# First quarter loads and splits of a seven-product mixing stage issued under the end of the stage before it

## The chip, the cores and the metric

The kernel runs on one NeuronCore of a Trainium2 chip. The metric is the device time of one execution in microseconds (us). Engines are named as in the profile: PE (TensorE matmul), PEld (its weight loads), DVE (VectorE), ACT (ScalarE), POOL (GpSimd) and SP (SyncE, which here only issues transfers).

## The reference

Three blocks follow each other, all in float32 (cut to what matters):

```python
Y = soft_threshold(rfft(x, axis=1) @ W + b)            # complex W, lam = 0.01
x = irfft(Y, n=3072, axis=1)                           # (4, 3072, 256)
h = relu(x @ w_in); u, v = h[..., :512], h[..., 512:]
v_n = (v - mean(v)) / sqrt(var(v) + 1e-6)
v_s = einsum('ts,bsd->btd', w_spatial, v_n) + b_spatial[None, :, None]
x = ((u * v_s) @ w_out).reshape(4 * 3072, 256)
out = (s * relu(x @ w2_in) ** 2 + b) @ w2_out          # 2048 hidden columns
```

## The kernel before

Every float32 operand of a product is split into a high and a low half (`_hl` tiles), and a product is three passes: high by high, high by low, low by high. ACT casts the high half, DVE subtracts to get the low half.

The program has three stages, written one after the other; each engine gets its instructions in the order of the Python code, and nothing reorders them.

`attention` is the filter: a 3072-point transform in steps (`s1`, `g_stage`), the channel product (`mix`), and two inverse steps (`g2_stage`, `s3`). Beside the last inverse step `s3` runs `v_product`, which makes the 96 row blocks of `v` (tile `vr`; the product's PSUM tile is `ps_vp`), normalises them three at a time (`bn`, `rs`, L583 to L601) and stores them to DRAM as `vn`. When the main loop is over, 40 of the 128 `s3` steps are left; the loop at L678 to L685 does them with the remaining `v_product`s. I call it the **tail**. In it SP issues the loads `v_f` (L276) and the stores `yd` (L465), POOL the stores `vn`.

`mixing` multiplies the 3072x3072 matrix with `vn` by a seven-product scheme on 2x2 blocks, nested twice: 7 outer times 7 inner products of 6 steps, 294 steps `n` of 24 matmuls (L834) each. Operands are kept as quarters, SBUF tiles `a11` to `b22`, six pieces each (`a` pieces 384 KB, `b` pieces 256 KB). Lines L858 and L859 issue the first 48 piece loads. A step's operands are split two steps ahead (`high`, `low`), three splits are held (`bufs=3`), and sums of quarters (`sums`) are made three steps ahead. The accumulators `acc` take all eight PSUM banks: `acc` 0 stands where `ps_g` was, 1 where `pm` was, 2 on `pa`, 3 on `py`; `v_product` of the tail uses `pm` and `pa`. Between steps one of 40 weight pieces is converted from float64 (`convert_half`, tiles `c_w`: a load on SP, nine DVE operations L143 to L158, one ACT copy L155, a store `cd`); every third step may start one, and it is worked off two steps later (L887 to L891).

`output` forms 16 blocks: it sums the outer products read back from DRAM (`combine`, tiles `m`), multiplies by `u` (`u_product`, L983 and L986), and runs the two layers (L1020, L1041). Its 20 weight tiles `w` come from `cd`; before, POOL issues all of them at L917, behind its stores of `md`.

Of the kernel before, what the change touches and what calls it, by code (L numbers as in the profile page):

```python
# [19 lines left out]
NB = 4  # L20
# [204 lines left out]
    return float(np.array([bits], np.uint32).view(np.float32)[0])  # L225


def attention(tc, nc, x, w_r, w_i, b_r, b_i, c_f, c_b, c_g, c_v, c_s, zd, vd, yd, vn, chunks, cd, nb=NB):


    left, right = Pools(tc, "left"), Pools(tc, "right")
# [6 lines left out]
    pg = left("a_pg", 1, space=PSUM)  # L238
    pm = left("a_pm", 2, space=PSUM)
    pa = left("a_pa", 2, space=PSUM)  # L240
    py = left("a_py", 2, space=PSUM)
    ch = Chains()

    cf = const.tile([N1, 2 * N1], F32R, name="cf")
# [237 lines left out]
    y_hl = {}  # L482
    chunks_ready = [0]

    root = const.tile([128, 1], F32, name="root")
    nc.vector.memset(root, 1.0)
    nc.scalar.sqrt(root, root)
    nc.gpsimd.dma_start(out=cf, in_=c_f)
# [181 lines left out]
    def s3_more():  # L670
        nonlocal s3_done
        if s3_done < 32 * nb:
# [14 lines left out]
    right.close()  # L687
    left.close()

# [16 lines left out]
FIRST_USE = {"a12": 0, "b21": 0, "a21": 1, "a22": 1, "b12": 1, "b11": 1, "a11": 2, "b22": 2}  # L706


def mixing(tc, nc, ws, vn, md, sd, convert_half):


# [1 line left out]

    left, right = Pools(tc, "left"), Pools(tc, "right")
    ring = left("m_ring", 3)
    stage = left("m_stage", 2)
    quarters = left("m_quarters", 1)
    keep = right("m_keep", 1)
    accs = left("m_acc", 1, space=PSUM)
    q = {}  # L720
    QUARTERS = ("a11", "a12", "a21", "a22", "b11", "b12", "b21", "b22")
    for name in ("a12", "b21", "a21", "a22", "b12", "b11", "b22", "a11"):
        n = TQ if name[0] == "a" else 512
        for i in range(NS):
            q[name, i] = quarters.tile([128, n], F32, tag=f"{name}{i}", name=name)
    PASSES = ((0, 0), (0, 1), (1, 0))
    outer = list(OUTER)

# [12 lines left out]
    def load(g, name, i):  # L741
        first, then = OUTER[outer[g]][0 if name[0] == "a" else 2:][:2]
        t = q[name, i]
        nc.sync.dma_start(out=t, in_=source(first, name, i))
        if then is None:
            return
        op, second, kept = then
        n = t.shape[1]
        s = stage.tile([128, n], F32, tag="st_" + name[0], name="st_" + name[0], bufs=3)
# [31 lines left out]
    def sums(n):  # L781

        p, i = INNER[n // NS % 7], n % NS
        a11, a12, a21, a22, b11, b12, b21, b22 = (q[x, i] for x in QUARTERS)
        if p == 2:
            a, b = a12, b21
        elif p == 5:
            add(a21, a21, a22)
            sub(b12, b12, b11)
            a, b = a21, b12  # L790
        elif p == 3:
            sub(a21, a21, a11)
            a, b = ring.tile([128, TQ], F32, tag="s4", name="s4", bufs=2), b22
            sub(a, a12, a21)
        elif p == 1:
            a, b = a11, b11
        elif p == 6:
            sub(b12, b22, b12)
            sub(b11, b12, b11)
            sub(b22, b21, b12)  # L800
            a, b = a21, b12
        elif p == 7:
            sub(a21, a22, a21)
            a, b = a21, b11
        else:
            a, b = a22, b22
        term["a", n], term["b", n] = a, b
# [13 lines left out]
            todo.extend((g + 1, FIRST_USE[x], n % NS, x) for x, last in LAST.items() if last == at)  # L821

    acc = {}

    def multiply(n):
        p, i = INNER[n // NS % 7], n % NS
        a, b = hl.pop(("a", n)), hl.pop(("b", n))
        fresh = p in (2, 5, 1, 4)
        for d in range(4):
            if i == 0 and fresh:  # L830
                acc[d] = accs.tile([128, 2, 512], F32, tag=f"acc{d}", name="acc")
# [6 lines left out]
    kept = {}  # L838

    def keep_tile(k, d):  # L840
        return keep.tile([128, 2, TH], F32, tag=f"k{k}{d}", name="kept")

    def evacuate(n, d):
        g, at = divmod(n // NS, 7)
# [10 lines left out]
            nc.scalar.copy(t, ps)  # L855

    total = len(outer) * 7 * NS
    for n in sorted(((u, i, x) for x, u in FIRST_USE.items() for i in range(NS))):  # L858
        load(0, n[2], n[1])  # L859
    for n in range(2):  # L860
        sums(n)
        for kind in "ab":
            high(kind, n)
            low(kind, n)
    sums(2)
    conversion = []
    for n in range(total):
        now[0] = n
        multiply(n)
        ends = n % NS == NS - 1  # L870
        if n + 2 < total:
            high("a", n + 2)
            high("b", n + 2)
        if n + 3 < total:
            sums(n + 3)
        if ends:
            evacuate(n, 0)
            evacuate(n, 1)
        if n + 2 < total:
            low("a", n + 2)  # L880
            low("b", n + 2)
            freed(n + 2)
        if ends:
            evacuate(n, 2)
            evacuate(n, 3)
        outer_sums(3)
        if conversion and (todo or n % 3 == 2):  # L887
            conversion.pop()()
        loads()
        if not conversion and not added and not todo and n % 3 == 0:  # L890
            conversion = [x for x in [convert_half(stage)] if x]  # L891
    while True:
        for x in conversion:
            x()
        conversion = [x for x in [convert_half(stage)] if x]
        if not conversion:
            break
    left.close()
    right.close()


def output(tc, nc, yd, md, chunks, cd, bs, s_in, b_in, out):


    left, right = Pools(tc, "left"), Pools(tc, "right")
    late = left("o_late", 2)
    mpool = left("o_m", 9)
    work = left("o_work", 2)
    wts_late = right("o_wl", 1)
# [120 lines left out]
    def layer2(n, k):  # L1030
        s = sq_t.pop((n, k))
        if k == 0:
            oacc[n] = accs.tile([128, 2, 512], F32, tag="oacc", name="oacc")
        ps = oacc[n]
        for e in range(2):
            ff = 2 * k + e
            w = w2[8 + ff // 2]
            for h in range(2):
                o = (ff % 2) * 256 + h * 128
                for c, (a, i) in enumerate(PASSES):  # L1040
                    nc.tensor.matmul(ps[:, h, 0:TH], w[:, a, o:o + 128], s[:, i, e, :],  # L1041
                                     start=ff == 0 and c == 0, stop=ff == 2 * NP - 1 and c == 2)
        if k == NP - 1:
            del oacc[n]
            b, o = where(n)
            t = work.tile([128, 2, TH], F32, tag="o_sb", name="o_sb")
# [26 lines left out]
    wo = [weight(4 + k) for k in range(2)]  # L1073
    w2 = [weight(6 + j) for j in range(16)]
# [8 lines left out]
    load_terms(1)  # L1083
    fetch(1)
    out_product(0)
    sums = combine(1)
    steps = [(n, k) for n in range(len(blocks)) for k in range(NP)]
# [35 lines left out]
def network(ctx, tc, ins, out):  # L1123
# [24 lines left out]
        return lambda: [step() for step in convert(nc, c_tile, raw, cd[j][:, :, h * 256:(h + 1) * 256], 256)]  # L1148
    with tc.manual_schedule():
        attention(tc, nc, ins['x'], ins['w_r'], ins['w_i'], ins['b_r'], ins['b_i'],  # L1150
                  ins['c_f'], ins['c_b'], ins['c_g'], ins['c_v'], ins['c_s'], zd, vd, yd, vn, chunks, cd)
        mixing(tc, nc, ins['moe_w_spatial'], vn, md, sd, convert_half)
        output(tc, nc, yd, md, chunks, cd, ins['moe_b_spatial'], ins['moe2_s'], ins['moe2_b'], out)


# [23 lines left out]
```

## Time and profile before

| what | us |
|---|---|
| median of 3 runs | 3241.53 (3240.82 to 3249.85) |
| the profiled execution, its own time | 3237.02 |
| its span, first to last instruction | 3235.2 |
| PE busy | 3090.4 (96%) |
| DVE busy | 2306.8 (71%) |

The span is 1.8 us shorter than the execution's own time, which is 4.5 us under the median. PE is close to full on average; where it is not is read from its timeline. The tail runs from about 475 to 562 us, `mixing` from 569 to 1856 us, `output` from there to the end.

### The profile page before, as it was taken

Reading aid. Unit: us, or ns where it says so; the run is one execution under the profiler, and the core shown is the slowest. Engines: PE = TensorE matmul, PEld = TensorE weight load, DVE = VectorE, ACT = ScalarE, POOL = GpSimd, SP = SyncE. Lnnn points to the kernel's source line nnn. Section 1 sums busy time; section 2 is a strip of 40 time slices with the busy share of each in tenths; the row PEclk is TensorE's granted clock in tenths of the full one; section 3 lists DMA queues with packets and bytes.
Section 4 is the critical chain, followed back from the end, with each engine's and each line's share of the span. In section 5 each row is a group of like instructions: output and inputs, shape, how many; then the busy total and the mean of one; then the engine's idle time right before and its main releaser. Section 6 shows DMA issues by size and latency. Waiting matters only on the chain.

```text
span 3235.2 us, 46499 instructions
## 1 busy us (share of the span) xinstructions
PE 3090.4 (96%) x17960; PEld 3013.2 (93%) x17960; DVE 2306.8 (71%) x3493; ACT 1426.1 (44%) x2241; POOL 396.3 (12%) x508
## 2 busy tenths in 40 slices
PE   7989997798999999999999989999999999999999
PEld 5888985798999999999999979999999999999999
DVE  4877988687878888888878655556666666656564
ACT  4776766333434333443434333444444444444433
POOL 2665534012000210000000100000000000000000
PEclk9999999899999999999999999999999999999999
DMA  7987655689465966467471441111111111110210
GB/s 232 290 266 226 225 178 201 228 289 365 137 208 161 341 248 220 163 198 277 141 250 33 156 140 50 64 54 64 54 64 54 64 54 64 49 65 29 72 44 15
DMA packets 230518, 488.30 MB, mean 151 GB/s; under 512 B 22356, under 2 KB 116376, under 8 KB 230296
## 3 DMA queue, kind: packets, MB, share of 16 engines
q1 hardware_dynamic: 195528, 347.67, 32.4%
q0 software_dynamic: 34768, 137.67, 11.6%
q8 instruction: 140, 2.29, 0.3%
q14 instruction: 82, 0.67, 0.1%
HBM read 322.72 MB, written 162.53 MB: 150 GB/s over the span
## 4 chain that ended last, share of the span: by engine, by line
PE 44%; issue 39%; DVE 8%; POOL 4%; ACT 3%; DMA 1%; POOLq 0%; SPq 0%; ACTq 0%; DVEq 0%
PE oacc L1041 15%; PE ps_h L1020 14%; PE ps_o L1001 4%; PE ps_u L983 4%; PE ps_m L406 3%; PE ps_vp L570 2%; POOL md L852 2%; DVE m L951 1%; DVE r L1025 1%; PE ps_z L332 1%; ACT q_hl L1026 1%; POOL s L755 1%; POOL t L755 1%; PE ps_g L359 1%; PE ps_y L454 1%
## 5 line engine op out<-in xcount | busy, mean ns | idle before, releaser
L834 PE MATMUL acc<-a_hl,b_hl 128*128 128x384 f32 x7056 | 1240.7, 337 | 52.7 <-ACT b_hl L812 25.2
L834 PEld LDWEIGHTS acc<-a_hl,b_hl 128*128 128x128 f32 x7056 | 1234.3, 189 | 59.2 <-ACT b_hl L812 25.9
L1020 PE MATMUL ps_h<-x_hl,w 128*128 128x384 f32 x3072 | 576.7, 337 | 1.6 <-ACT x_hl L1004 0.9
L1041 PE MATMUL oacc<-q_hl,w 128*128 128x384 f32 x3072 | 576.3, 337 | 0.0
L1020 PEld LDWEIGHTS ps_h<-x_hl,w 128*128 128x128 f32 x3072 | 538.2, 188 | 2.5 <-ACT x_hl L1004 1.2
L1041 PEld LDWEIGHTS oacc<-q_hl,w 128*128 128x128 f32 x3072 | 538.5, 188 | 0.2
L812 ACT CAST a_hl<-a 128x768 fp32r<-128x768 f32 x252 | 210.9, 837 | 532.2 <-PE acc L834 450.3
L1027 DVE TENSOR_TENSOR q_hl<-r,q_hl 128x768 fp32r<-128x768 f32 x256 | 245.3, 958 | 230.8 <-ACT q_hl L1026 230.8
L1025 DVE TENSOR_TENSOR r<-r 128x768 f32<-128x768 f32 x256 | 244.7, 956 | 216.0 <-ACT r L1024 216.0
L1026 ACT CAST q_hl<-r 128x768 fp32r<-128x768 f32 x256 | 213.8, 835 | 314.3 <-DVE r L1025 314.3
L1024 ACT ACTIVATE r<-ps_h 128x768 f32<-128x768 f32 x256 | 207.7, 811 | 301.7 <-PE ps_h L1020 300.6
L816 DVE TENSOR_TENSOR a_hl<-a,a_hl 128x768 fp32r<-128x768 f32 x252 | 240.3, 953 | 134.9 <-ACT a_hl L812 133.6
L816 DVE TENSOR_TENSOR b_hl<-b,b_hl 128x512 fp32r<-128x512 f32 x294 | 201.0, 684 | 0.0
L812 ACT CAST b_hl<-b 128x512 fp32r<-128x512 f32 x294 | 181.1, 616 | 0.0
L570 PE MATMUL ps_vp<-win,y_hl 128*128 128x512 f32 x576 | 155.2, 406 | 18.3 <-ACT v_sb L437 15.0
L983 PE MATMUL ps_u<-y_hl,w 128*128 128x384 f32 x768 | 148.7, 344 | 21.6 <-DVE m L986 14.2
L852 POOL DMA_DIRECT2D md<-kept x112 | 60.4, 540 | 827.6 <-DVE kept L851 823.6
L983 PEld LDWEIGHTS ps_u<-y_hl,w 128*128 128x128 f32 x768 | 137.2, 193 | 25.3 <-DVE m L986 16.7
L1001 PE MATMUL ps_o<-g,w 128*128 128x384 f32 x768 | 140.0, 338 | 1.7 <-DVE g L991 1.1
L570 PEld LDWEIGHTS ps_vp<-win,y_hl 128*128 128x128 f32 x576 | 103.1, 192 | 40.5 <-ACT v_sb L437 16.8
L1001 PEld LDWEIGHTS ps_o<-g,w 128*128 128x128 f32 x768 | 134.0, 188 | 2.7 <-DVE g L991 1.6
L990 ACT CAST g<-m 128x768 fp32r<-128x768 f32 x64 | 53.4, 835 | 157.0 <-DVE m L986 134.1
(138 smaller groups left out, 3749.8 us busy)
## 6 DMA issues: line engine op xcount, KB each, us to landing
a<-in_moe_w_spatial_dram SPq DMA_DIRECT2D x144, 384.0 KB, 4.8
b<-vn SPq DMA_DIRECT2D x168, 256.0 KB, 6.1
md<-kept POOLq DMA_DIRECT2D x112, 384.0 KB, 5.5
m<-md SPq DMA_DIRECT2D x56, 768.0 KB, 5.9
st_a<-in_moe_w_spatial_dram SPq DMA_DIRECT2D x72, 384.0 KB, 6.4
vn<-vr POOLq DMA_DIRECT2D x96, 256.0 KB, 3.8
s<-a POOLq DMA_DIRECT2D x48, 384.0 KB, 5.9
x_f<-in_x_dram SPq DMA_DIRECT2D x32, 384.0 KB, 5.8
```

The source lines that it names most:

```text
L570: nc.tensor.matmul(ps, y[:, a, k, o:o + 128], win[k][:, w, :], start=c == 0, stop=c == 5)
L812: nc.scalar.copy(s[:, 0, :], t)
L816: sub(s[:, 1, :], term.pop((kind, n)), f(s)[:, 0, :])
L834: nc.tensor.matmul(acc[d][:, h, 0:TH], b[:, m, d * 128:(d + 1) * 128], a[:, w, h * TH:(h + 1) * TH], start=fresh and i == 0 and c == 0, st ...
L983: nc.tensor.matmul(ps[:, d, 0:TH], win[k][:, a, o:o + 128], y[:, w, k, :], start=c == 0, stop=c == 5)
L1001: nc.tensor.matmul(ps[:, h, 0:TH], wo[k // 2][:, a, o:o + 128], g[:, w, k, :], start=c == 0, stop=c == 11)
L1020: nc.tensor.matmul(ps[:, e, 0:TH], w[:, a, o:o + 128], x[:, i, j, :], start=c == 0, stop=c == 5)
L1024: nc.scalar.activation(r, ps[:, :, 0:TH], AF.Relu)
L1025: nc.vector.tensor_mul(r, r, r)
L1026: nc.scalar.copy(s[:, 0], r)
L1027: nc.vector.tensor_sub(s[:, 1], r, f(s)[:, 0])
L1041: nc.tensor.matmul(ps[:, h, 0:TH], w[:, a, o:o + 128], s[:, i, e, :], start=ff == 0 and c == 0, stop=ff == 2 * NP - 1 and c == 2)
```

## The change

`mixing` is called from inside `attention` and returns an object with three parts. `prefetch` issues one quarter load per turn of the tail loop, 36 of the 48 (all but `a11` and `b22`), into the left side of SBUF, which `attention` closes before its tail. `split_first` sums and splits one step's operands; the tail loop calls it on each turn that ends with 93 or 95 row blocks of `v` started. `run` does the rest. The first conversion is started at step 6 and not at step 0. In `output` the weights `w2` to `w12` move from POOL's queue to SP's, seven of them into space that the quarters of the last product held, and `split(0)` is written ahead of `combine(0)`.

```diff
     tail[0] = True
+    left.close()
+    stage = follow()
     while v_done[0] < NV:
+        stage.prefetch()
         s3_more()
...
+        if v_done[0] in (NV - 3, NV - 1):
+            stage.split_first()
     ch.flush()
     right.close()
-    left.close()
+    banks.close()
+    return stage
...
+    first = sorted((u, i, x) for x, u in FIRST_USE.items() for i in range(NS))
+    begun = [0]
+
+    def prefetch():
+        if first and first[0][2] != "a11":
+            _, i, x = first.pop(0)
+            load(0, x, i)
+
+    def split_first():
+        n = begun[0]
+        begun[0] += 1
         sums(n)
         for kind in "ab":
             high(kind, n)
             low(kind, n)
...
+        while begun[0] < 2:
+            split_first()
+        while first:
+            _, i, x = first.pop(0)
+            load(0, x, i)
+        sums(2)
...
-        if not conversion and not added and not todo and n % 3 == 0:
+            if n >= 6 and not conversion and not added and not todo and n % 3 == 0:
...
     def weight(j):
-        t = (wts_late if j >= 13 else wts).tile([128, 2, 512], F32R, tag=f"w{j}", name=f"w{j}")
-        nc.gpsimd.dma_start(out=t, in_=cd[j])
+        pool = wts_late if j >= 13 else wts_mid if j >= 6 else wts
+        t = pool.tile([128, 2, 512], F32R, tag=f"w{j}", name=f"w{j}")
+        (nc.gpsimd if j >= 13 else nc.sync).dma_start(out=f(t) if j < 13 else t, in_=cd[j])
...
-    load_terms(0)
     fetch(0)
     win = [weight(2 + k) for k in range(2)]
+    load_terms(0)
     wo = [weight(4 + k) for k in range(2)]
...
+    split(0)
     for step in combine(0):
         step()
-    split(0)
```

What SP issues in the tail before, from its middle to the first quarter loads of `mixing`:

```order
L465 DMA yd_68<-y_sb 128x2x384
L276 DMA v_f<-vd_64 96x512 x2
L465 DMA yd_68<-y_sb 128x2x384 x3
L744 DMA a_7447<-in_moe_w_spatial_dram 128x768
L744 DMA b_7453<-vn_69 128x512
```

And in the changed program, one period of the same tail:

```order
L466 DMA yd_68<-y_sb 128x2x384
L758 DMA a_6332<-in_moe_w_spatial_dram 128x768
L758 DMA b_6368<-vn_69 128x512
L277 DMA v_f<-vd_64 96x512
L758 DMA b_6362<-vn_70 128x512
L758 DMA a_6357<-in_moe_w_spatial_dram 128x768
L277 DMA v_f<-vd_64 96x512
L466 DMA yd_68<-y_sb 128x2x384
```

Four quarter loads now stand in each period of two `v_f` loads and one `yd` store. The second place is ACT at the end of the tail, before; the `vr` rows of L608 empty the PSUM tiles of the last `v_product`s:

```order
L608 ACTIVATE vr<-ps_vp 128x512
L611 ACTIVATE rs<-rs 128x3
L608 ACTIVATE vr<-ps_vp 128x512
L599 ACTIVATE vr<-vr,rs 128x512 x2
L608 ACTIVATE vr<-ps_vp 128x512 x2
```

ACT at the same place in the changed program, where the numbers of `a` tell the step:

```order
L609 ACTIVATE vr<-ps_vp 128x512
L826 CAST a_hl<-a_6343 128x768
L826 CAST b_hl<-b_6349 128x512
L612 ACTIVATE rs<-rs 128x3
L826 CAST a_hl<-a_6344 128x768
L826 CAST b_hl<-b_6350 128x512
L609 ACTIVATE vr<-ps_vp 128x512
L600 ACTIVATE vr<-vr,rs 128x512 x2
L609 ACTIVATE vr<-ps_vp 128x512
L826 CAST a_hl<-a_6345 128x768
L826 CAST b_hl<-b_6351 128x512
L609 ACTIVATE vr<-ps_vp 128x512
```

Three pairs of casts have moved ahead of the last three `vr` rows (the loop passes the 93 mark twice and the 95 mark once); the third pair, `a_6345`, is cast again later, since `run` splits step 2 itself. The third place is DVE at the start of `output`, before:

```order
L851 TENSOR_TENSOR kept<-acc,kept 128x768 x4
L1075 MEMSET ones 128x2
L951 TENSOR_TENSOR m<-m 128x768
L953 TENSOR_TENSOR m<-m,bias 128x768
L951 TENSOR_TENSOR m<-m 128x768
L953 TENSOR_TENSOR m<-m,bias 128x768
L969 TENSOR_TENSOR y_hl<-y_f,y_hl 128x768
L986 SCALAR_TENSOR_TENSOR m<-ps_u,m 128x768
```

DVE there in the changed program:

```order
L866 TENSOR_TENSOR kept<-acc,kept 128x768 x4
L1116 MEMSET ones 128x2
L1008 TENSOR_TENSOR y_hl<-y_f,y_hl 128x768
L990 TENSOR_TENSOR m<-m 128x768
L992 TENSOR_TENSOR m<-m,bias 128x768
L990 TENSOR_TENSOR m<-m 128x768
L992 TENSOR_TENSOR m<-m,bias 128x768
L1025 SCALAR_TENSOR_TENSOR m<-ps_u,m 128x768
```

The low half of `y` now comes before the four sums of `m`; the eight rows are otherwise the same.

## Rows read from the trace of the kernel before

**Rows 1.** Timeline of PE, 555 to 650 us: start, length, what [idle before].

```profile
558.24 3.94 PE L570 MATMUL ps_vp<-win,y_hl 128*128 128x512 f32 x16 [0.26 <-DVE y_hl L475]
569.11 22.94 PE L834 MATMUL acc<-a_hl,b_hl 128*128 128x384 f32 x120 [6.94 <-ACT b_hl L812]
...
610.28 1.01 PE L834 MATMUL acc<-a_hl,b_hl 128*128 128x384 f32 x2 [18.23 <-ACT b_hl L812]
612.13 38.12 PE L834 MATMUL acc<-a_hl,b_hl 128*128 128x384 f32 x204 [0.84 <-DVE a_hl L816]
```

**Rows 2.** Timeline of PE, the last stretch of mixing.

```profile
1607.08 248.50 PE L834 MATMUL acc<-a_hl,b_hl 128*128 128x384 f32 x1428 [0.73 <-DVE kept L851]
```

**Rows 3.** Timeline of ACT around the second gap.

```profile
608.57 0.41 ACT L155 CAST c_w<-c_w 128x256 fp32r<-128x256 f32 x1 [27.61 <-DVE c_w L149]
608.88 0.83 ACT L812 CAST a_hl<-a 128x768 fp32r<-128x768 f32 x1
609.62 0.61 ACT L812 CAST b_hl<-b 128x512 fp32r<-128x512 f32 x1
```

**Rows 4.** Timeline of DVE around the second gap.

```profile
607.05 0.29 DVE L143 TENSOR_SCALAR c_w<-c_w 128x256 uint32<-128x256 uint32 x1 [25.02 <-DMA c_w<-in_moe_w_in_dram]
...
609.65 0.95 DVE L788 TENSOR_TENSOR a<-a,a 128x768 f32<-128x768 f32 x1
```

**Rows 5.** Timeline of SP's queue: first quarter load, first conversion load.

```profile
556.76 0.50 SPq L744 DMA_DIRECT2D a<-in_moe_w_spatial_dram  x1
...
600.71 0.33 SPq L128 DMA_DIRECT2D c_w<-in_moe_w_in_dram  x1
```

**Rows 6.** Stretches: length, busy PE, PEld, DVE, ACT, POOL; PE clock, DMA share, GB/s.

```profile
475.00:557.00 82.00, 66.23 (x345) 50.97 (x344) 71.87 (x215) 55.11 (x125) 39.62 (x48) 1.00 0.53 180
...
570.00:600.00 30.00, 22.05 (x119) 21.73 (x117) 6.25 (x9) 4.28 (x7) 0.00 (x0) 0.90 1.04 400
...
612.00:620.00 8.00, 7.87 (x31) 7.77 (x32) 7.93 (x16) 4.53 (x8) 0.00 (x0) 0.65 0.16 28
```

**Rows 7.** Timeline of PE, first matmuls of output.

```profile
1862.28 1.30 PE L983 MATMUL ps_u<-y_hl,w 128*128 128x384 f32 x3 [6.70 <-DMA w<-cd]
```

**Rows 8.** Timeline of POOL, first weight loads of output.

```profile
1857.44 4.37 POOL L917 DMA_DIRECT2D w<-cd  x8
```

**Rows 9.** Timeline of DVE, start of output.

```profile
1856.50 0.95 DVE L951 TENSOR_TENSOR m<-m 128x768 f32<-128x768 f32 x1
...
1860.22 0.95 DVE L969 TENSOR_TENSOR y_hl<-y_f,y_hl 128x768 fp32r<-128x768 f32 x1
1867.06 0.96 DVE L986 SCALAR_TENSOR_TENSOR m<-ps_u,m 128x768 f32<-128x768 f32 x1 [5.88 <-PE ps_u L983]
```

**Rows 10.** Timeline of ACT at the end of the tail.

```profile
557.10 0.59 ACT L608 ACTIVATE vr<-ps_vp 128x512 f32<-128x512 f32 x1
...
561.14 1.52 ACT L599 ACTIVATE vr<-vr,rs 128x512 f32<-128x512 f32 x2 [1.07 <-DVE rs L595]
562.56 1.06 ACT L608 ACTIVATE vr<-ps_vp 128x512 f32<-128x512 f32 x2
```

**Rows 11.** Timeline of DVE at the end of the tail.

```profile
559.04 0.17 DVE L587 TENSOR_SCALAR rs<-mv 128x3 f32<-128x3 f32 x1
...
560.88 0.16 DVE L595 SCALAR_TENSOR_TENSOR rs<-mv,rs 128x3 f32<-128x3 f32 x1
```

**Rows 12.** One of the page's costliest groups: count | busy, mean ns | idle before.

```profile
L816 DVE TENSOR_TENSOR b_hl<-b,b_hl 128x512 fp32r<-128x512 f32 x294 | 201.0, 684 | 0.0
```

**Rows 13.** Timeline of SP's queue, the last conversion's store.

```profile
1785.44 0.52 SPq L161 DMA_DIRECT2D cd<-c_w  x1
```

**Rows 14.** Timeline of DVE late in mixing, end of a product.

```profile
1802.23 2.00 DVE L851 TENSOR_TENSOR kept<-acc,kept 128x768 f32<-128x768 f32 x2 [1.11 <-PE acc L834]
```

**Rows 15.** DMA issues, 475 to 557 us: count, size, median us to landing.

```profile
yd<-y_sb SPq DMA_DIRECT2D x11, 384.0 KB, 2.5
v_f<-vd SPq DMA_DIRECT2D x16, 192.0 KB, 2.7
```

More of the change, by code (lines that the diff above doesn't have):

```diff
@@ L225, in _as_float, with attention @@
     return float(np.array([bits], np.uint32).view(np.float32)[0])
-def attention(tc, nc, x, w_r, w_i, b_r, b_i, c_f, c_b, c_g, c_v, c_s, zd, vd, yd, vn, chunks, cd, nb=NB):
-    left, right = Pools(tc, "left"), Pools(tc, "right")
+def attention(tc, nc, x, w_r, w_i, b_r, b_i, c_f, c_b, c_g, c_v, c_s, zd, vd, yd, vn, chunks, cd, follow, nb=NB):
+    left, right, banks = Pools(tc, "left"), Pools(tc, "right"), Pools(tc, "left")
     raws = left("a_raw", 3)
@@ L237, in attention @@
     vpool = right("a_v", 2)
[L238 to L241, printed above, removed]
+    pg = banks("a_pg", 1, space=PSUM)
+    pm = banks("a_pm", 2, space=PSUM)
+    pa = banks("a_pa", 2, space=PSUM)
+    py = banks("a_py", 2, space=PSUM)
     ch = Chains()
@@ L483, in attention @@
     chunks_ready = [0]
-    root = const.tile([128, 1], F32, name="root")
+    root = s3c.tile([128, 1], F32, name="root")
     nc.vector.memset(root, 1.0)
@@ L706, with __init__ @@
 FIRST_USE = {"a12": 0, "b21": 0, "a21": 1, "a22": 1, "b12": 1, "b11": 1, "a11": 2, "b22": 2}
+class Stage:
+    def __init__(self, prefetch, split_first, run):
+        self.prefetch, self.split_first, self.run = prefetch, split_first, run
 def mixing(tc, nc, ws, vn, md, sd, convert_half):
@@ L715, in mixing, with place @@
     ring = left("m_ring", 3)
-    stage = left("m_stage", 2)
     quarters = left("m_quarters", 1)
-    keep = right("m_keep", 1)
-    accs = left("m_acc", 1, space=PSUM)
     q = {}
     QUARTERS = ("a11", "a12", "a21", "a22", "b11", "b12", "b21", "b22")
[L722 to L725, printed above, removed]
+    def place(pool, names):
+        for name in names:
+            n = TQ if name[0] == "a" else 512
+            for i in range(NS):
+                q[name, i] = pool.tile([128, n], F32, tag=f"{name}{i}", name=name)
+    place(quarters, ("a22", "b22", "a12", "b21", "a21", "b12", "b11"))
     PASSES = ((0, 0), (0, 1), (1, 0))
@@ L748, in load @@
         n = t.shape[1]
-        s = stage.tile([128, n], F32, tag="st_" + name[0], name="st_" + name[0], bufs=3)
+        s = banks[2].tile([128, n], F32, tag="st_" + name[0], name="st_" + name[0], bufs=3)
         nc.sync.dma_start(out=s, in_=source(second, name, i))
@@ L783, in sums @@
         p, i = INNER[n // NS % 7], n % NS
-        a11, a12, a21, a22, b11, b12, b21, b22 = (q[x, i] for x in QUARTERS)
+        a11, a12, a21, a22, b11, b12, b21, b22 = (q.get((x, i)) for x in QUARTERS)
         if p == 2:
@@ L823, in mixing @@
     acc = {}
+    banks = []
     def multiply(n):
@@ L830, in multiply @@
             if i == 0 and fresh:
-                acc[d] = accs.tile([128, 2, 512], F32, tag=f"acc{d}", name="acc")
+                acc[d] = banks[0].tile([128, 2, 512], F32, tag=f"acc{d}", name="acc")
             for c, (m, w) in enumerate(PASSES):
@@ L840, in keep_tile @@
     def keep_tile(k, d):
-        return keep.tile([128, 2, TH], F32, tag=f"k{k}{d}", name="kept")
+        return banks[1].tile([128, 2, TH], F32, tag=f"k{k}{d}", name="kept")
     def evacuate(n, d):
@@ L864, in mixing @@
             low(kind, n)
[L865 to L889, printed above, removed]
-        if not conversion and not added and not todo and n % 3 == 0:
-            conversion = [x for x in [convert_half(stage)] if x]
@@ L892, in mixing, with run @@
[L892 to L899, printed above, removed]
+    def run():
+        banks.append(left("m_acc", 1, space=PSUM))
+        banks.append(right("m_keep", 1))
+        place(left("m_a11", 1), ("a11",))
+        banks.append(left("m_stage", 2))
+        stage = banks[2]
+        while begun[0] < 2:
[4 more added lines that the diff above has]
+        sums(2)
+        conversion = []
+        for n in range(total):
+            now[0] = n
+            multiply(n)
+            ends = n % NS == NS - 1
+            if n + 2 < total:
+                high("a", n + 2)
+                high("b", n + 2)
+            if n + 3 < total:
+                sums(n + 3)
+            if ends:
+                evacuate(n, 0)
+                evacuate(n, 1)
+            if n + 2 < total:
+                low("a", n + 2)
+                low("b", n + 2)
+                freed(n + 2)
+            if ends:
+                evacuate(n, 2)
+                evacuate(n, 3)
+            outer_sums(3)
+            if conversion and (todo or n % 3 == 2):
+                conversion.pop()()
+            loads()
+            if n >= 6 and not conversion and not added and not todo and n % 3 == 0:
+                conversion = [x for x in [convert_half(stage)] if x]
+        while True:
+            for x in conversion:
+                x()
+            conversion = [x for x in [convert_half(stage)] if x]
+            if not conversion:
+                break
+        left.close()
+        right.close()
@@ L902, in output @@
+    return Stage(prefetch, split_first, run)
 def output(tc, nc, yd, md, chunks, cd, bs, s_in, b_in, out):
@@ L906, in output @@
     late = left("o_late", 2)
+    wts_mid = left("o_wm", 1)
+    outs = left("o_out", 2)
     mpool = left("o_m", 9)
@@ L1045, in layer2 @@
             b, o = where(n)
-            t = work.tile([128, 2, TH], F32, tag="o_sb", name="o_sb")
+            t = outs.tile([128, 2, TH], F32, tag="o_sb", name="o_sb")
             for h in range(2):
@@ L1150, in network @@
         attention(tc, nc, ins['x'], ins['w_r'], ins['w_i'], ins['b_r'], ins['b_i'],
-                  ins['c_f'], ins['c_b'], ins['c_g'], ins['c_v'], ins['c_s'], zd, vd, yd, vn, chunks, cd)
-        mixing(tc, nc, ins['moe_w_spatial'], vn, md, sd, convert_half)
+                  ins['c_f'], ins['c_b'], ins['c_g'], ins['c_v'], ins['c_s'], zd, vd, yd, vn, chunks, cd,
+                  lambda: mixing(tc, nc, ins['moe_w_spatial'], vn, md, sd, convert_half)).run()
         output(tc, nc, yd, md, chunks, cd, ins['moe_b_spatial'], ins['moe2_s'], ins['moe2_b'], out)
```

7 lines of the change are left out of this document (2 added, 5 removed).

## Prediction

> **What bounds the kernel now.** PE is close to full on average, so I read its timeline for the places where it is not, and asked at each what ended the wait. There are two such places near the edit, with three gaps.
>
> At the seam from the tail to `mixing` [rows 1], the last `v_product` ends at 562.18 us. PE then idles 6.94 us until the first split is cast, does 120 matmuls (five steps), idles 18.23 us at 592 to 610, and 0.84 us more. The reader should see that the long gap is not the first one and that it comes after five steps of work. The pace of an undisturbed stretch is 248.50 us for 1428 matmuls, 0.174 us each or 4.18 us a step [rows 2].
>
> What ends the long gap is named as an ACT cast, but ACT itself had stood for 27.61 us in the copy of a conversion [rows 3], because DVE had stood for 25.02 us in the first operation of that conversion, waiting for its load [rows 4]. That load was issued at 600.71 us, and SP had issued nothing but quarter loads from 556.76 to then [rows 5]: the conversion's load stood behind all 48. In the middle of that queue the DMA share is 1.04 at 400 GB/s [rows 6], so the transfers themselves fill the time. Thus the wait is a small side job, issued at step 0 and worked off at step 2, that blocks ACT and DVE until all 48 pieces (15.7 MB) have passed.
>
> After the gap PE also runs slow: the granted clock is 0.65 on average in 612 to 620 [rows 6], part of it at 1.2 GHz and part at 2.4, after PE had stood still. The 206 matmuls behind the gap take 39.13 us [rows 1]; at the pace of [rows 2] they would take 35.8. That is 3.3 us.
>
> At the seam from `mixing` to `output`, PE idles 6.70 us and is released by a weight load [rows 7]. POOL issues the weights at 1857.44, behind its stores of the last product [rows 8]. DVE meanwhile does four sums and the low half of `y` from 1856.50 to 1861.17, then waits 5.88 us for PE's first half of `u` until 1867.06 [rows 9].
>
> **The change part by part.** *The long gap.* The conversion at step 0 is gone (first one at step 6), and 36 of the 48 loads are issued under the tail, so nothing at step 3 waits for data. What then holds steps 5 and 6 is DVE: the sums of the second product are two operations of 0.95 and 0.7 us [rows 4, 12] and its splits the same again, 3.3 us against 4.18 us a step. PE need not wait. Gain 18.23 + 0.84 idle and 3.3 clock: 22.4 us. Bounds: 19.1 if the slow clock stays, 24 if the half-speed start of the first five steps goes too (22.94 us for 120 matmuls, where 20.9 is the pace).
>
> *The first gap.* Here I disagree with what the splits under the tail seem to give. Operands are ready early, but the accumulators are not: `acc` 1 takes both `pm` banks, and the last `v_product` lies in one of them. Before, ACT had emptied that tile at 563.62 [rows 10]. Now the three pairs of casts stand on ACT ahead of its last rows. Worked forward: `vr` 92 ends at 557.7; a pair takes 1.35 us (608.88 to 610.23 [rows 3]), to 559.0; the square root then waits for DVE, where the pair's low halves (0.95 and 0.7 us less overlap, about 1.5) now stand ahead of the operation that was at 559.04 [rows 11], so 560.9; second pair to 562.3, `vr` 93 to 562.8. DVE has the second pair's low halves until 563.4, then the rescale chain, which needed 559.48 to 561.04 before (1.6 us after the root, ending in [rows 11]): 565.0. ACT's two normalisations wait for that, 1.52 us, to 566.5; `vr` 94 to 567.1; third pair to 568.3; `vr` 95 to 568.9. So PE can do the quarter of step 0 that goes to `acc` 0 (6 matmuls, 1.0 us) right after 562.2 and stands until about 569.0, where it started at 569.11 before. Gain 1.1 us. Bounds: 7.9 us if the accumulator is freed as early as it was (the full gap and 1.0), and a loss of 2 us if ACT's order costs more than I counted. I take 1.1, since each link is a row.
>
> *The seam to `output`.* SP now issues `w2` to `w5` behind the last conversion's store. That store was issued at 1785.44 [rows 13]; two conversions are left out at the start and made at the end instead, two times three steps of 4.18 us, so about 25 us later, still 45 us ahead of the seam. The seven weights that lie where the last product's quarters were need the splits of the last step, which are made two steps (8 us) ahead. So no weight is late. PE's first product then needs the low half of `y`, which DVE does first at 1856.5 (ready 1857.4), and 12 matmuls of 0.174 end at 1859.5. DVE's four sums end later: 3.72 us (1856.50 to 1860.22 [rows 9]) after 1857.4 is 1861.1, and there the product with `u` starts, instead of 1867.06. Gain 5.9 us. Bounds: 0 if another wait takes the place, 7.5 if the sums were not in front.
>
> *The two conversions at the end* cost DVE 2.6 us each (607.05 to 609.65 [rows 4]). Late in `mixing` DVE arrives at the end of the product and waits 1.11 us for PE [rows 14]; with 2.6 us more it is 1.5 us late, of which about 1 is covered, since the next step comes to accumulators 2 and 3 only 2 us in. Cost 0.5 us, bounds 0 and 2.6. The third split is made twice: 1.35 us of ACT and 1.6 of DVE while PE is busy with step 0, no cost.
>
> *The moved loads in the tail.* 18 of 384 KB and 18 of 256 KB, 11.8 MB; at 400 GB/s [rows 6] 29.5 us of all engines. The tail's 82 us are 0.53 full [rows 6], 43 us; together 73 of 82. It fits, without much room. PE's and DVE's work paces the tail (DVE busy 71.87 of 82 [rows 6]). A `yd` store lands after 2.5 us, a `v_f` load after 2.7 [rows 15]. Four `s3` steps last 8.2 us (82 us for 40) and `y_sb` has two buffers, so a store may be some 5.7 us late before anything waits; two quarter loads ahead of it are 2 us. I take 0.5 us, bounds 0 and 30. The Trainium skill, page "DMA: Bandwidth & Descriptors", section "Queues, rings and completion order", says that what one sequencer issues is consumed in order on each ring, so quarter loads do go ahead of the tail's own. No row here shows it apart. By the rows the delay stays in the slack and the sum as it is; by the rule alone each of the 36 loads could be a delay, and the sum would be that of the third rival.
>
> *Sum.* 22.4 + 1.1 + 5.9 - 0.5 - 0.5 = 28.4 us. The profiled execution took 3237.0 us and becomes 3208.6. The median of the runs shown is 4.5 us above it, so on its scale 3241.5 - 28.4 = 3213.
>
> **The rivals.** *The first gap closes too.* For it: the splits are ready. Against it: the order on ACT above. Time 3213 - 6.8 = 3206. Chance 0.12.
>
> *The seam to `output` keeps its wait.* The place of the weight load is taken by another space or sum on which DVE or SP stands. Against it: the space is given up 8 us earlier. Time 3219. Chance 0.1.
>
> *The tail pays for each moved load* (the other side). Each of the 36 loads, issued ahead of a `v_f` or `yd`, would push it back by its own transfer, and the tail grows by all 29.5 us: 3243, no change. It turns slower where each of the ten `yd` stores of the tail lands 3.8 us beyond its slack of 5.7, 38 us in all: 3251. That needs some 3.8 MB ahead of each store, and an average of 1.2 MB is issued between two. Against it is also the share of 0.53. Chance 0.04 slower, 0.04 the same.
>
> *The long gap only shrinks,* since something else stands in the same order (a quarter that has not landed, a sum). Say half of it stays: 3224. Chance 0.08.
>
> **How the numbers follow.** My own forecast, 3213 give or take 4, has 0.62. Two in ten are left out by a range from 3204 (first gap closed) to 3222 (a seam without gain, or 8 us lost in the tail). Within 0.3% of 3241.5 is 9.7 us, about what runs of one kernel scatter here. Faster by more than that means under 3231.8: all cases but the third rival, 0.92; the same 0.04; slower 0.04.
>
> **What would show it.** Right: no idle of PE over 1 us from step 0 to 20 of `mixing`; 6 matmuls of `acc` right behind the last `ps_vp`, then a wait of some 5.8 us released by ACT (L609), not by a cast (L826); the first `u` product within 2 us of the last `acc`, with DVE's L1025 about 5.9 us sooner after the last `kept`; 475 to 562 as long as before with a DMA share near 0.9. Wrong: the tail longer by several us with PE waiting for DVE's `y_sb` or for a `v_f`; a wait of PE in steps 3 to 8 for a quarter's DMA; a new wait late in `mixing` for `kept`.

## Result and the profile after

The changed kernel takes 3213.4 us (median of 4 runs, 3211.0 to 3214.0) where the kernel before takes 3241.2 on the same chip (4 runs, 3240.8 to 3249.9): 27.8 us less. The ratio of the means of the runs is 0.9906, with a 95% interval of 0.9889 to 0.9924. One run of the kernel before in the third group of experiments below took 4334.7 us, at a granted clock of 0.66, and is left out of all figures there. The profiled executions take 3237.0 and 3213.5 us, only 23.5 apart: the one of before lies 4.2 us under its median, the one of after on it. That matters below, since the sum of the terms is checked against the profiles.

The ends of the last `ps_vp`, the last `acc` and the last `oacc`, and the start of the first `oacc`, cut both profiled spans into five stretches (us, from PE's rows; forecast from the terms of the sum):

| stretch | before | after | change | forecast |
|---|---|---|---|---|
| start to the last `ps_vp` | 562.2 | 563.2 | +1.0 | +0.5 |
| to the last `acc` (all of `mixing`) | 1293.4 | 1270.2 | -23.2 | -23.0 |
| to the first `oacc` (seam) | 28.4 | 23.9 | -4.6 | -5.9 |
| to the last `oacc` (output, steady) | 1346.6 | 1349.2 | +2.7 | 0 |
| to the end | 4.7 | 5.0 | +0.3 | 0 |

The timeline of PE in the changed kernel where the tail meets `mixing`, against [rows 1]: start, length, what, and in brackets the idle time before it with its releaser.

```profile
559.28 3.94 PE L571 MATMUL ps_vp<-win,y_hl 128*128 128x512 f32 x16 [0.26 <-DVE y_hl L476]
563.06 1.22 PE L849 MATMUL acc<-a_hl,b_hl 128*128 128x384 f32 x6
569.49 90.74 PE L849 MATMUL acc<-a_hl,b_hl 128*128 128x384 f32 x509 [5.21 <-ACT vr L609]
```

The reader should see one gap where there were three. Six matmuls of the first step run straight behind the tail; then PE waits for an `acc` bank and for ACT's copy of a `vr`, no longer for a cast; and then 509 matmuls pass without a break where before there were 120, 2 and 204 with 18.23 and 0.84 us between.

The timeline of ACT in the same place, against [rows 10], shows why the first gap is still there:

```profile
558.14 0.59 ACT L609 ACTIVATE vr<-ps_vp 128x512 f32<-128x512 f32 x1
558.63 0.82 ACT L826 CAST a_hl<-a 128x768 fp32r<-128x768 f32 x1
...
561.62 0.20 ACT L612 ACTIVATE rs<-rs 128x3 f32<-128x3 f32 x1 [1.64 <-DVE rs L588]
561.73 0.82 ACT L826 CAST a_hl<-a 128x768 fp32r<-128x768 f32 x1
...
565.71 1.52 ACT L600 ACTIVATE vr<-vr,rs 128x512 f32<-128x512 f32 x2 [2.15 <-DVE rs L596]
567.13 0.57 ACT L609 ACTIVATE vr<-ps_vp 128x512 f32<-128x512 f32 x1
567.61 0.82 ACT L826 CAST a_hl<-a 128x768 fp32r<-128x768 f32 x1
...
568.85 0.59 ACT L609 ACTIVATE vr<-ps_vp 128x512 f32<-128x512 f32 x1
```

The last row, at 568.85, empties the last PSUM tile of the tail; PE goes on at 569.49. Between this row and the one at 558.14 stand the three pairs of casts and two waits for DVE.

Two stretches of the changed kernel (length, then busy time and count of PE, PEld, DVE, ACT and POOL, then PE's granted clock, DMA share, GB/s), against [rows 6]:

```profile
475.00:557.00 82.00, 67.17 (x352) 51.93 (x350) 71.68 (x215) 54.69 (x125) 38.79 (x47) 1.00 0.91 321
...
570.00:600.00 30.00, 30.00 (x163) 30.00 (x162) 21.00 (x38) 13.41 (x20) 1.60 (x3) 0.93 0.48 169
```

and the tail's DMA issues in 475 to 557 us (count, size, median us from issue to landing), against [rows 15]:

```profile
yd<-y_sb SPq DMA_DIRECT2D x10, 384.0 KB, 4.4
v_f<-vd SPq DMA_DIRECT2D x16, 192.0 KB, 6.8
```

The tail's DMA share has gone from 0.53 to 0.91 and a `v_f` load lands after 6.8 us instead of 2.7, yet DVE is as busy as before (71.68 us against 71.87) and PE does a little more (67.17 against 66.23).

The timeline of all engines at the seam to `output`, against [rows 7, 9]:

```profile
1833.23 0.34 PE L1022 MATMUL ps_u<-y_hl,w 128*128 128x384 f32 x1
1834.31 0.95 DVE L1008 TENSOR_TENSOR y_hl<-y_f,y_hl 128x768 fp32r<-128x768 f32 x1
...
1835.32 4.33 PE L1022 MATMUL ps_u<-y_hl,w 128*128 128x384 f32 x23 [1.75 <-DVE y_hl L1008]
...
1838.90 0.95 DVE L1025 SCALAR_TENSOR_TENSOR m<-ps_u,m 128x768 f32<-128x768 f32 x1
...
1844.49 4.63 PE L1040 MATMUL ps_o<-g,w 128*128 128x384 f32 x17 [0.55 <-DVE g L1030]
```

No weight is waited for. DVE's first product with `u` follows its sums without idle time, 5.5 us behind the last `acc` (1833.4) where it came 11.5 us behind it before (1855.6 to 1867.06). But the 17 matmuls of `ps_o` take 4.63 us; at the pace of [rows 2] they would take some 3. The granted clock is 0.88 in 1836 to 1850 us, so part of them ran at 1.2 GHz. Which matmuls of this seam run slow differs from profile to profile, as the experiment on the split shows.

### The profile page after: what moved, and what is told of

Read it like the earlier page. It is cut to its first block, busy times and chain, and to the rows that moved or that the text cites. A ratio compares the mean times of both kernels' runs of the same rounds, so it can differ in the third digit from the quotient of the medians.

```text
span 3211.4 us, 46502 instructions
## 1 busy us (share of the span) xinstructions
PE 3094.6 (96%) x17960; PEld 3017.5 (94%) x17960; DVE 2307.1 (72%) x3495; ACT 1428.1 (44%) x2243; POOL 391.0 (12%) x497
## 4 chain that ended last, share of the span: by engine, by line
PE 63%; issue 17%; DVE 12%; ACT 3%; DMA 3%; POOL 2%; SPq 0%; POOLq 0%; ACTq 0%; DVEq 0%
PE acc L849 18%; PE ps_h L1059 15%; PE oacc L1080 15%; PE ps_o L1040 4%; PE ps_u L1022 4%; PE ps_m L407 3%; PE ps_vp L571 2%; DVE m L990 1%; DVE r L1064 1%; ACT q_hl L1065 1%; PE ps_z L333 1%; PE ps_g L360 1%; POOL md L867 1%; POOL s L769 1%; DMA vd<-v_sb 1%
## 5 line engine op out<-in xcount | busy, mean ns | idle before, releaser
L849 PE MATMUL acc<-a_hl,b_hl 128*128 128x384 f32 x7056 | 1239.4, 336 | 30.9 <-DVE kept L866 13.1
```

## Experiments

The theory is the one of the prediction: the long gap was the conversion's load behind 48 quarter loads; the early splits cannot close the first gap, for an `acc` bank is missing; the seam paid for weights issued late; the loads in the tail cost nothing. Rivals: the loads are what closes the long gap, or the tail pays for them; the output's new order does nothing. The steady output, 2.7 us slower, was a question of its own. Medians, and intervals of the ratio of the means, in three groups of runs, each with its own runs of before. The first group ran on one chip and the others on another, so medians compare within a group:

| kernel | median, us | ratio to before, 95% |
|---|---|---|
| before beside it | 3236.7 | |
| late conversion alone | 3214.2 | 0.9916 to 0.9941 |
| no early splits | 3216.8 | 0.9923 to 0.9950 |
| splits behind the tail | 3210.6 | 0.9902 to 0.9929 |
| no early loads | 3215.8 | 0.9923 to 0.9948 |
| before beside it | 3239.1 | |
| middle weights on the right | 3213.1 | 0.9901 to 0.9929 |
| middle weights by POOL | 3213.0 | 0.9903 to 0.9930 |
| old output | 3217.2 | 0.9914 to 0.9941 |
| conversion at the start | 3221.3 | 0.9927 to 0.9957 |
| before beside it | 3237.5 | |
| changed kernel again | 3211.4 | 0.9904 to 0.9934 |
| middle weights last | 3213.7 | 0.9915 to 0.9941 |
| splits behind, weights last | 3211.5 | 0.9902 to 0.9931 |
| split after the sums | 3215.9 | 0.9920 to 0.9946 |

**Late conversion alone.** The kernel before, with one condition added:

```
-        if not conversion and not added and not todo and n % 3 == 0:
+        if n >= 6 and not conversion and not added and not todo and n % 3 == 0:
```

> The kernel before with one edit: the first conversion starts at step 6 and not at step 0; no load, split or weight moves. Theory (the long gap is DVE and ACT standing in a small job whose load is queued behind 48 others, while the quarters themselves arrive in time): the second gap goes nearly whole, 22 us less than before, 3219 us; the 6.9 us gap and the 6.7 us gap stay. Rival (the gap is the transfers, 15.7 MB at 400 GB/s, and only issuing them earlier helps): PE still idles over 10 us near step 5, released by a quarter's load, and the time is 3231 us or more.

It came out 22.5 us faster than the runs of before beside it. PE's timeline at the start of `mixing` and at the seam, and between them the stretch of [rows 6] in which the 48 loads run:

```profile
568.01 77.25 PE L834 MATMUL acc<-a_hl,b_hl 128*128 128x384 f32 x433 [6.96 <-ACT b_hl L812]
...
1840.67 1.30 PE L983 MATMUL ps_u<-y_hl,w 128*128 128x384 f32 x3 [7.25 <-DMA w<-cd]
```

```profile
570.00:600.00 30.00, 30.00 (x168) 30.00 (x168) 18.75 (x25) 12.20 (x18) 0.00 (x0) 0.96 1.04 400
```

The DMA is as full as before (1.04, 400 GB/s), and PE does not wait for one quarter. So the long gap was the conversion's place and nothing else; the first gap and the seam's wait stay, as they should. `mixing` takes 1272.4 us, 21.0 less than before.

**No early loads, no early splits, splits behind the tail.** The changed kernel, without the loads in the tail (and so without the splits there); with the loads and without the splits; and with both splits moved out of the loop. In the first, `run` then also issues all the loads ahead of its first splits, which the lines here leave out; the second takes out only the last two lines:

```
     while v_done[0] < NV:
-        stage.prefetch()
...
-        if v_done[0] in (NV - 3, NV - 1):
-            stage.split_first()
...
```

The third:

```
         if s3_done == 32 * nb:
             ch.step()
-        if v_done[0] in (NV - 3, NV - 1):
-            stage.split_first()
+    stage.split_first()
+    stage.split_first()
     ch.flush()
```

> The changed kernel without loads and splits under the tail; all 48 loads are issued when the tail is over, the first conversion still starts at step 6, and output is the changed one. Theory (the early loads are not what removed the long gap): as without early splits, within 1 us of 3214.5 us, tail DMA share back at 0.53. Rival (they are): 20 us more, 3234 us.

> The changed kernel without the splits under the tail; loads under the tail stay. Theory (the splits only let a quarter of step 0 run early, since ACT empties the last PSUM tile late): first matmul of acc at about 570 us released by a cast, 1 us more than the changed kernel, 3214.5 us. Rival (the early splits close the first gap): 3219 us or more.

> The changed kernel with the two early splits written right behind the tail loop, so that on ACT their casts follow the rows that empty the last PSUM tiles and stand ahead of the last square root. Theory (it is ACT's order that keeps the first gap): first full step starts at about 565 to 566 us on the changed kernel's time axis and not at 569.5, the wait shrinks to about 3 us, 3.5 to 5.5 us less than the changed kernel, 3209 us. Rival (something else holds acc, such as DVE's chain or another bank): no difference, 3213 us.

PE's timeline at the start of `mixing`, without the loads, without the splits, and with the splits behind the tail:

```profile
571.35 73.89 PE L846 MATMUL acc<-a_hl,b_hl 128*128 128x384 f32 x412 [6.94 <-ACT b_hl L823]
```

```profile
570.34 74.92 PE L847 MATMUL acc<-a_hl,b_hl 128*128 128x384 f32 x422 [5.82 <-ACT b_hl L824]
```

```profile
565.96 0.62 PE L849 MATMUL acc<-a_hl,b_hl 128*128 128x384 f32 x2 [2.75 <-ACT b_hl L826]
566.83 78.36 PE L849 MATMUL acc<-a_hl,b_hl 128*128 128x384 f32 x440 [0.26 <-DVE a_hl L830]
```

The first two take the same time within their runs: with the conversion late, the early loads give nothing that shows, and cost nothing. From the end of the last `ps_vp` to the last `acc` they take 1272.6 and 1270.9 us, the changed kernel 1270.2, the third 1268.5. In the third the rows that empty PSUM stand ahead of the casts, the wait is 2.75 us instead of 5.21, and its median, 3210.6, is the lowest of its group. The changed kernel did not run in this group; against its profile `mixing` is 1.7 us shorter, where 3.5 to 5.5 were expected. What the early splits were worth lay in where they stand, not in how early they are.

**Conversion at the start.** The changed kernel with the conversion's old condition:

```
-            if n >= 6 and not conversion and not added and not todo and n % 3 == 0:
+            if not conversion and not added and not todo and n % 3 == 0:
```

> The changed kernel with the conversion again starting at step 0, the loads of the quarters left under the tail. Theory: the early loads would have closed the long gap alone, since the conversion's load then stands behind only about 12 loads that land by about 588 us: at most a few us of wait, 3213 to 3217 us (0.991 to 0.992); the two edits are two ways to the same gain, and together no more than either. Rival: only the later start closes the gap: DVE waits for c_w as before (some 18 us), PE waits behind it, and the time is 3231 to 3235 us (0.997).

It lies between the two, 3221.3 us. The timelines of SP's queue, DVE and PE:

```profile
575.97 0.34 SPq L758 DMA_DIRECT2D a<-in_moe_w_spatial_dram  x1
...
584.26 0.33 SPq L128 DMA_DIRECT2D c_w<-in_moe_w_in_dram  x1
```

```profile
590.44 0.29 DVE L143 TENSOR_SCALAR c_w<-c_w 128x256 uint32<-128x256 uint32 x1 [10.97 <-DMA c_w<-in_moe_w_in_dram]
```

```profile
593.66 1.01 PE L849 MATMUL acc<-a_hl,b_hl 128*128 128x384 f32 x2 [4.18 <-ACT b_hl L826]
595.51 30.85 PE L849 MATMUL acc<-a_hl,b_hl 128*128 128x384 f32 x166 [0.83 <-DVE a_hl L830]
```

The first theory counted the 12 loads as if SP could issue them at once; SP issues the first at 575.97, 20 us behind the last `yd` store. Its wait of 20.2 us ends with a `vn` store (`vn<-vr`): the space of these loads is given up only then. DVE stands 10.97 us for `c_w` instead of 25.02, PE 4.18 instead of 18.23, and `mixing` takes 1278.2 us, 8 more than in the changed kernel. So either edit removes most of the long gap, only the later start removes all of it, and their gains do not add.

**Old output, split after the sums.** The changed kernel with the whole old `output`; and with `split(0)` behind `combine(0)` again. (The old `output` also keeps its results in another pool and fetches the second block's operands later, which the diff shown with the change leaves out.) The second edit:

```
-    split(0)
     for step in combine(0):
         step()
+    split(0)
```

> The changed kernel with the whole output function of the kernel before: old placement, loaders and order. Theory: the wait at the seam comes back (5.9 us, PE behind DMA of w), the half-clock matmuls of ps_o (1.3 us) go, and the ps_h pace is 2.08 us again (4 to 5 us back): 3214 us (0.991), so the output's new order is worth almost nothing as it stands. Rival (the slower pace does not come from the output function but from what ran ahead of it): the pace stays 2.11 us and the time is 3218 us (0.9925).

> The changed kernel with the output's first split of y behind the first sums again, as in the kernel before (the early loads and the other order stay). Theory: DVE makes the low half of y only after two sums and two bias additions (about 3.6 us), so the first u products start late, and the seam from the last acc matmul to the first oacc matmul is about 2 us longer: 3215 us, 2 us above the changed kernel on the same chip. Rival: the sums would have been waited for anyway by the first multiplication with m, so nothing changes: 3213 us.

PE's timeline at the seam, with the old output, and with the split after the sums:

```profile
1840.52 1.30 PE L1019 MATMUL ps_u<-y_hl,w 128*128 128x384 f32 x3 [6.61 <-DMA w<-cd]
```

```profile
1838.63 6.75 PE L1022 MATMUL ps_u<-y_hl,w 128*128 128x384 f32 x23 [5.47 <-DVE y_hl L1008]
```

With the old output the wait for `w` is back, and the kernel takes 3217.2 us beside 3213.1 and 3213.0 of the two with the new order: the new output as a whole is worth some 4 us, not 5.9. The pace of the `ps_h` groups (next experiment) is 2.08 us again, as expected, but the steady output, at 1346.5 us, is only 2.7 us shorter than in the changed kernel, where 4 to 5 were expected.

With the split after the sums PE stands 5.47 us instead of 1.75, and the granted clock behind it is 0.62 in 1838 to 1846 us. The first product with `u` (L1025) comes 9.6 us behind the last `acc`. Before it is 11.5, and in all ten profiles that have the split first (the changed kernel's two and those of eight other edits) it is 5.5. So this one line carries 4.1 of the 6.0 us that the new order gives up to there. The expectation of 2 had the wait, and left out that the matmuls behind it run slow.

What of this reaches the first `oacc` depends on where the slow clock falls. The seam lasts 28.3 us here and 22.4 to 26.3 in those ten. PE at the seam in the changed kernel's second profile, and with the middle weights last (below); the order is the same:

```profile
1834.94 5.82 PE L1022 MATMUL ps_u<-y_hl,w 128*128 128x384 f32 x23 [1.75 <-DVE y_hl L1008]
...
1844.10 3.22 PE L1040 MATMUL ps_o<-g,w 128*128 128x384 f32 x17 [0.55 <-DVE g L1030]
```

```profile
1833.58 4.26 PE L1022 MATMUL ps_u<-y_hl,w 128*128 128x384 f32 x23 [1.75 <-DVE y_hl L1008]
...
1842.75 5.51 PE L1040 MATMUL ps_o<-g,w 128*128 128x384 f32 x17 [0.30 <-DVE g L1030]
...
1850.20 7.93 PE L1059 MATMUL ps_h<-x_hl,w 128*128 128x384 f32 x35 [0.55 <-DVE x_hl L1044]
```

The first seam lasts 22.4 us and the second 26.3. The medians lie likewise: 3215.9 us with the split after the sums is 4.5 more than the changed kernel beside it, and 2.2 more than the kernel with the middle weights last.

**Middle weights on the right, by POOL, last.** Three placements of `w6` to `w12` in the changed kernel: in the pool where they were before, still loaded by SP (the pool that falls empty goes too, not shown); at the new place, loaded by POOL with a cast; and above the sums on the left:

```
-        pool = wts_late if j >= 13 else wts_mid if j >= 6 else wts
+        pool = wts_late if j >= 13 else wts
```

```
-        (nc.gpsimd if j >= 13 else nc.sync).dma_start(out=f(t) if j < 13 else t, in_=cd[j])
+        (nc.gpsimd if j >= 6 else nc.sync).dma_start(out=f(t) if j < 6 else t, in_=cd[j])
```

```
     late = left("o_late", 2)
-    wts_mid = left("o_wm", 1)
     outs = left("o_out", 2)
     mpool = left("o_m", 9)
     work = left("o_work", 2)
+    wts_mid = left("o_wm", 1)
```

> The changed kernel, with the seven weight tiles w6 to w12 of the output stage back in the pool on the right side of SBUF where the kernel before had them; they are still loaded by SP without a cast. It asks why each ps_h group of 12 matmuls starts 2.11 us after the one ahead of it ends its part (2.08 us in the kernel before and in the late-conversion one). Theory: the place of the weights (or of what moved up behind them) slows the first four matmuls of each group by 26 ns; then the pace is 2.08 us here, and 250 groups of some 20 ns give 4 to 5 us back: 3209 us (0.9895). Rival: it is the loader (SP, no cast); then the pace stays 2.11 us and the time 3213 us (0.991).

> The changed kernel, with w6 to w12 at their new place on the left side but loaded by POOL with the cast, as in the kernel before. Theory (the place): the pace of ps_h stays 2.11 us, 3213 us (0.991). Rival (the loader): 2.08 us and 3209 us (0.9895).

> The changed kernel with w6 to w12 still on the left side and loaded by SP, but laid above the sums and work tiles instead of directly above x_hl, r and q_hl. Theory: what slows the first matmuls of each ps_h group (185, 176, 181 ns against 174) is where these weights lie beside the tiles that ACT and DVE read and write at that moment; away from them the middle ps_h group is 2080 ns again. Because the kernels with the weights on the right have stretches of 32 oacc groups at 2120 ns, some 3.3 us each, the time may stay within 2 us of the changed kernel all the same: 3208 to 3214 us. Rival: any place on the left does it, and the middle group stays 2105 ns, 3213 us.

PE's timeline in the steady output: the changed kernel, then the one with the weights on the right at two places.

```profile
2200.97 2.27 PE L1059 MATMUL ps_h<-x_hl,w 128*128 128x384 f32 x12
2203.07 2.25 PE L1080 MATMUL oacc<-q_hl,w 128*128 128x384 f32 x12
2205.16 2.27 PE L1059 MATMUL ps_h<-x_hl,w 128*128 128x384 f32 x12
2207.27 1.55 PE L1080 MATMUL oacc<-q_hl,w 128*128 128x384 f32 x8
```

```profile
2203.68 2.24 PE L1058 MATMUL ps_h<-x_hl,w 128*128 128x384 f32 x12
2205.76 2.24 PE L1079 MATMUL oacc<-q_hl,w 128*128 128x384 f32 x12
2207.84 2.24 PE L1058 MATMUL ps_h<-x_hl,w 128*128 128x384 f32 x12
...
2404.79 2.28 PE L1079 MATMUL oacc<-q_hl,w 128*128 128x384 f32 x12
2406.91 2.28 PE L1058 MATMUL ps_h<-x_hl,w 128*128 128x384 f32 x12
2409.03 2.28 PE L1079 MATMUL oacc<-q_hl,w 128*128 128x384 f32 x12
```

Read the distances between starts. In the changed kernel a `ps_h` group takes 2.10 to 2.11 us and an `oacc` group 2.08 to 2.09, everywhere. With the weights on the right both take 2.08 us at 2200 and 2.12 at 2404. The loader does not matter: by POOL the groups are 2.11 and 2.09 again. So the place of these seven tiles does decide the pace, as the theory said, but the gain that I expected did not come: 3213.1 us and 3213.0. In the profile with the weights on the right (the slowest of its six runs, 3216.3 us), 95 of 253 full `oacc` groups are of the slow kind, nearly all in three stretches of 30 to 32, and its steady output takes 1349.8 us, no less than the changed kernel's 1349.2. The kernel before has 57 slow groups in two stretches (1346.6 us), the old output 63 in two (1346.5), the late conversion alone 30 in one (1343.9): some 3 us for each stretch. My estimate from these four is some 1341 us with no such stretch, which no profile shows.

Laid above the sums, the weights give the same 2.11 and 2.09 us, though every other tile of the left side then lies where it does with the weights on the right: that it is what moved up behind them has fallen, and so have the neighbours that they had in the changed kernel. It is not simply the place of the tile that a matmul reads either: an `oacc` group reads only `w14` to `w21`, which lie on the right in every kernel, and its pace changes too. What it is about the weights on the left stays open.

**The changed kernel again, and splits behind with weights last.**

> The changed kernel as it stands, to stand beside the next three on one chip: 0.991 to 0.992 of the kernel before, about 3213 us, with ps_h groups of 2105 ns in the middle of the distribution and of the oacc groups at 2088 ns.

> The best of the edits together: the changed kernel with the two first splits issued behind the tail's loop instead of inside it (no 5.2 us wait after the first six acc matmuls; 2 to 3 us less) and the weights laid as in the kernel before this one in the list. Theory: 3208 to 3211 us, 2 to 3 us under the changed kernel on the same chip. Rival: the gain of the splits is lost to the weights' place, 3213 us.

3211.4 and 3211.5 us: on this chip the two cannot be told apart, though PE's gap is shorter in the second (2.73 us) and its `mixing` takes 1267.8 us beside 1269.4. What the changed order of the splits may give is inside what runs of one kernel scatter, and no version here is shown to beat the changed kernel.

## Why the prediction was right, point by point

- **The long gap (22.4 us, of 23.0 for `mixing`): right.** The stretch is 23.2 us shorter. The late conversion alone takes 21.0 us off it by its profile, and 22.5 off the whole by the medians. Of the two reasons that the prediction names side by side, "the conversion at step 0 is gone" carries it; "36 of the 48 loads are issued under the tail" is not needed. The upper bound of 24 was not reached: the first matmuls of `mixing` still run slow, 90.74 us for 509 where the pace of [rows 2] gives 88.6, at a granted clock of 0.93 in 570 to 600 us.
- **The first gap (1.1 us): right in its mechanism, near in size.** The chain on ACT, worked forward, was to empty `vr` 95 by 568.9 us; it does so from 568.85 to 569.44, in a tail that ends 1.0 us later. PE waits 5.21 us for L609, not for a cast, where 5.8 was forecast. With the six early matmuls that is a gain of some 1.7 us from the end of the tail. That the casts' place makes the wait is shown by moving them behind the tail: 2.75 us.
- **The seam (5.9 us): right up to the first product with `u`, left to the clock behind it.** L1025 comes 6.0 us sooner after the last `acc`. But the first `oacc` comes only 4.6 us sooner: the 17 matmuls of `ps_o` ran in 4.63 us after PE's waits of the seam. In the changed kernel's second profile they take 3.22 and the seam is 22.4 us long, a gain of 6.0; the longest of the ten seams with this order, 26.3, would be one of 2.1. The sum left this out; it had charged such a loss to the long gap alone.
- **The steady output (0 in the sum): missed.** The prediction moved the weights without a price for where they lie. The stretch is 2.7 us longer than before's and 5 us longer than in the late conversion alone, whose output is the old one; the three profiles of the old output lie at 1343.9 to 1346.6 us, all those of the new one at 1348.6 to 1350.2. That the place of the weights costs this is not shown: with the weights back on the right the new output takes 1349.8 us, three slow stretches included.
- **Two conversions at the end (0.5 us): no wait to be seen.** PE's idle time for DVE's `kept` in all of `mixing` is 13.1 us in both kernels.
- **The tail (0.5 us): small, as forecast, but its size is not shown.** The last `ps_vp` ends 1.0 us later, but over all the kernels here it ends anywhere from 560.4 to 565.2 us, with early loads at either end. With the quarter loads issued between the tail's own, a `v_f` load lands 4.1 us later. The Trainium skill, page "DMA: Bandwidth & Descriptors", section "Queues, rings and completion order", states that on each DMA engine the descriptors of a ring are consumed in order. The later landing agrees with it, though no run tells it apart from what a DMA share of 0.91 does by itself. That the delay stayed in the slack is shown by the kernel without early loads, which is no faster.
- **The scale.** The profiled change is 23.8 us of span against 28.4 in the sum: the half-speed `ps_o`, the output's pace and the 0.3 at the end make up 4.3 of the 4.6, and the tail most of the rest. The medians differ by more than the profiles, 27.8 us here and 26.0 for the changed kernel's second set of runs; here that is because the profiled run of before was 4.2 us faster than its median. Which stretch is longer in its other runs no trace here shows; the slow stretches of `oacc` groups with the weights on the right, some 3 us each, are one thing that varies from profile to profile. So the forecast of 3213 held in the medians with a sum that by the profiles is 4.6 us too high, and by the second set of runs 2.4: that it hit to half a microsecond is luck. The terms that carry it, the long gap and the seam up to `u`, are not.

## What to carry to other kernels

Ask of every wait what the late transfer is queued behind: what cost PE some 22 us was a small side job behind 48 loads, and one condition on its first step gave 22.5 us by itself, where the whole change, with its rebuilding of pools and loads, gives 26 to 28. Work pulled forward in time is only worth something if what it frees is the last thing missing; here the splits came early and pushed back the rows that empty PSUM. And when a change moves operands to another place, look at the pace of the steady loop too: here it changed by 4 to 25 ns a group, and the stretch of some 500 groups came out 2.7 us longer, more than half of what the seam had gained.

## What the runs showed of the hardware

- **PE's pace changed with the place of seven stationary tiles.** With `w6` to `w12` on the right, a group of 12 matmuls takes 2.08 us, but for stretches of some 30 `oacc` groups (150 to 165 us) at 2.12, at a granted clock of 1.00 in both: 160 us hold 916 matmuls in one and 905 in the other. Which stretches are slow differs from kernel to kernel; the one around 1900 to 2050 us is slow in all four profiles with the weights on the right. With the weights at either of two places on the left there are no such stretches, and each `ps_h` group takes 2.11 us. The extra lies in its first four matmuls: they start 178, 185, 176 and 181 ns after the one ahead of each, the others of the group mostly after 173 to 174. Neither cause was found.
- **The slow clock behind the same waits does not fall in the same place.** In the ten profiles with the new order of the seam PE waits 1.75 us there and then 0.1 to 1.2 us a few times. The 23 matmuls behind the first wait take 4.26 to 5.83 us, the 17 of `ps_o` 3.22 to 5.51, the next 35 of `ps_h` 6.33 to 7.94, and the seam as a whole 22.4 to 26.3. Its mean granted clock is 0.80 to 0.93.
